# A cycle of 32 scores with four projections, and one MLP job moved from behind the last sums into the attention

## The chip, the core and the metric

The kernel runs on one core of a Trainium2 chip. The metric is the device time of one execution in microseconds (us).

The engines are named as in the profile: PE does the matmuls, ACT (ScalarE) the exponentials, DVE (VectorE) copies and elementwise work, POOL (GpSimd) a little of that, SP issues the transfers. PE writes into PSUM, in banks of 128 x 512 numbers.

## The reference

Two layers of attention and a token-mixing MLP, each with a residual and a layer norm; 2048 tokens, 512 channels, 32 heads of 16 that share one key and value head.

```python
def _A_ref(x, wq, wk, wv, wo):
    q = (x @ wq).reshape(B, S, H, Dh)      # H = 32, Dh = 16
    k = x @ wk
    v = x @ wv
    scores = einsum("bhqd,bkd->bhqk", q, k) * (Dh ** -0.5)
    p = softmax(scores, axis=-1)
    o = einsum("bhqk,bkd->bhqd", p, v)
    return o.reshape(B, S, H * Dh) @ wo

def _B_ref(x, w1, b1, w2, b2):             # F = 1792
    h = layernorm(x)
    u = gelu(einsum("bsd,sf->bdf", h, w1) + b1)
    return einsum("bdf,fs->bsd", u, w2) + b2

for _ in range(2):
    x = x + _A_ref(layernorm(x), wq, wk, wv, wo)
    x = x + _B_ref(layernorm(x), w1, b1, w2, b2)
```

## The kernel before

**Scores and sums.** The attention of a layer is cut into 32 groups (4 heads by 512 queries). A group has 32 steps, each for 128 keys and two heads: two score matmuls into a PSUM pair `sc` (L900; three such pairs exist and are used in turn), an exponential on ACT into a tile `p` (L910), and the sums, matmuls of `p` with the values into the group's accumulator `acc` (L916; two rows of the program, four matmuls in the profile). Some scores are "copied": DVE copies `sc` into `p` first (L908), which frees the pair, and ACT takes the exponential from there. The accumulators of even and odd groups lie in two PSUM banks; the bank that the present group doesn't use is free for other products. When a group's sums are done, DVE empties the accumulator (`ev`, L818), a transfer brings that into `o` (L823), and a division (a reciprocal at L836 and three more operations on each of four columns) makes `hl`.

**What else PE does meanwhile.** Two kinds of other work are laid between scores and sums. A *projection* (`po`, L877) multiplies `hl` with `wo` for 128 tokens: 6 matmuls for two parts `hl`, or 3 (a short one) for one part; DVE adds the result to `x` (L885). Four projections come due at a time, after every fourth group; after those of a token block's last heads the rows of `x` are normalized for the MLP on DVE (L1105 to L1119). A *job* (`pu`, L1187) is one product of the MLP's first matrix, 12 matmuls in two halves (`first`, `second`), after which DVE adds it to `ua` (L1195) and splits the next weights `w` (L1172, L1174). All jobs that the attention doesn't take are done behind it, in `Mixer.rest`; `KEPT` sets how many are kept back for that.

**The order** is written as turns: tuples in which a number above zero computes so many scores (13 and 12: three and two, the last of them copied), 0 does the next part (a projection or half a job), and a number below zero sums so many steps. `Attention.run` takes one turn after the other; `Mixer.turn` chooses it by what is due. `COPIED` is a cycle of 16 steps with two parts, `DOUBLE` one of 32 with four halves (two jobs). After each group of sums in these, `mix.step` puts a limited amount of side work on DVE (division columns, normalization): `room` is the limit, 2.4 in `COPIED` and 1.0 in `DOUBLE`. Engines work through their instructions in the order in which this code emits them.

**Behind the sums** (`rest`), PE does the remaining jobs but eight (`pu_e`), then three of the eight in part (`pu_a`, `pu_m`), while the last `acc` is emptied, moved to `o` and divided (L858 to L860); then the last projections (`po_l`) need that division.

In the layer's late part, four projections come due at the steps 422, 550, 678, 806 and 934 (groups 13, 17, 21, 25, 29), where two `COPIED` cycles follow each other; at step 982 (group 30, and on into 31) four short projections take two `COPIED` cycles, and behind them there is only `PLAIN` (two scores, two sums) to the end of the attention. Two `pu_e` jobs are left for `rest`. Both layers have the same late part.

Of the kernel before, what the change touches and what calls it, by code (L numbers as in the profile page):

```python
# [20 lines left out]
NB = 4  # L21
QB = 512
NG = 8
NKT = S // P
# [8 lines left out]
KEPT = 6  # L33
# [4 lines left out]
WHOLE = (13, 0, 0, 13, -4, 13, -4, 13, -4)  # L38
LONG = (2, 0, 13, -4, 13, -4, 13, 0, 13, -4, 12, -4)
COPIED = (13, 0, 12, 0, 13, -4, 13, -4, 3, -4, 2, -4)  # L40
DOUBLE = (
    13, -4, 13, 0, 0, 13, -4, 13, -4, 13, -4, 13, 0, 13, -4, 13, -4, 12, 0, 13, -4, 13, -4,
)
SHORT = (2, 0, 3, -4, 3, -4)
TINY = (2, 0, 2, -4)
# [21 lines left out]
def kernel(  # L67
# [18 lines left out]
    def pool(name, bufs=1, side="left"):  # L86
        return tc.alloc_tile_pool(name=name, bufs=bufs, side=side, reuse_waits="tile")
# [9 lines left out]
    def bank(i, name):  # L97
        return ps.tile([P, QB], F32, tag=f"ac{i % 2}", name=name)
# [140 lines left out]
    class Proj:  # L239
# [113 lines left out]
        def turn(self, ts_):  # L353

            self.transposes(ts_)
            self.first_rows(ts_)
            self.second_rows(ts_)
# [279 lines left out]
        def later(self, att):  # L637
# [3 lines left out]
            def put(turn, parts):  # L641
                work.append((turn, parts, None))
# [139 lines left out]
    class Attention:  # L782
# [185 lines left out]
        def size(self, turn):  # L968
            return sum(k % 10 for k in turn if k > 0)
# [6 lines left out]
        def run(self, mix, proj):  # L976


            total = 2 * NKT * NG * NB
            guards = [2 * NKT * g for g in sorted({2 * FIRST[self.l], NG})] + [total]  # L980
            self.guards = guards
            later, guarded, flagged = proj.later(self), 0, 0

            rest = range(NB - 2 if self.l == 0 else NB - 1, NB)
            turn, queued = FIRST_TURN[self.l], False
            parts = [lambda i, b=b: proj.values(b, i) for b in rest]
            while self.scored < total:
                mix.chores(self)
                ahead = min(t for t in guards if t > self.scored)
                if ahead < total and self.scored >= ahead - 16 and flagged < ahead:  # L990
                    flagged = ahead
                    proj.flag(proj.flagged)
                if turn is None:
                    turn = PLAIN
                    self.lag = 2 * LAG if mix.normed and self.scored < total - 16 else LAG
                    if len(self.pend) == self.lag:
                        after, queued = None, bool(later) and not mix.projections
                        if queued:
                            turn, parts, after = later[0]
                            if turn is WHOLE and self.to_boundary() >= 14 and self.slack(later) >= 4:  # L1000
                                turn = LONG
                        else:
                            turn, parts = mix.turn(self)
                            if turn is COPIED and not self.spares:
                                turn = LONG
                    left = min(t - self.scored for t in guards if t > self.scored)
                    if queued and turn is LONG and left < self.size(LONG):
                        turn = WHOLE
                    if left < self.size(turn):
                        turn = PLAIN  # L1010
                        if parts and mix.projections and left >= sum(k for k in SHORT if k > 0):
                            turn, parts = SHORT, parts[:1]
                    if turn in (LONG, COPIED) and self.to_boundary() in (2, 4, 2 * NKT):
                        turn = PLAIN
                    if turn is WHOLE and self.to_boundary() == 2:
                        turn = PLAIN
                parts = list(parts)
                for k in turn:
                    if k > 0:
                        self.more(mix, k)  # L1020
                    elif k == 0:
                        if queued and turn is TINY:
                            mix.step(2.0, self)
                        parts.pop(0)(self.spare())
                        if turn is DOUBLE and len(parts) % 2:
                            mix.step(1.0, self)
                        if queued and not parts:
                            later.pop(0)
                            if after:
                                after()  # L1030
                            if not later:
                                proj.close()
                                mix.open()
                    else:
                        if turn is PLAIN:
                            k = -min(4, max(0, len(self.pend) - self.lag))
                        end = self.to_boundary() <= -k
                        busy = self.behind
                        if busy:
                            self.behind = None  # L1040
                            busy()
                        self.drain(-k)
                        mix.chores(self)
                        if busy and turn is not DOUBLE:
                            continue
                        if self.pieces:
                            self.pieces.pop(0)()
                        elif turn in (LONG, COPIED, DOUBLE, WHOLE):
                            room = 2.4 if turn is COPIED else 1.0
                            mix.step(min(room, 0.8 * self.to_boundary()), self)  # L1050
                        elif end:
                            mix.step(2.0, self)
                assert self.scored < guards[-2] or not later
                if self.scored in guards[:-1] and self.scored > guarded:
                    guarded = self.scored
                    i = guards.index(guarded)
                    proj.guard(guarded // (2 * NKT), guards[i + 1] // (2 * NKT))
                    if mix.opened:
                        self.spares = pool(f"more{self.l}")
                if turn is PLAIN and self.to_boundary() > 4:  # L1060
                    mix.step(2.4, self)
                turn = None


    class Mixer:
# [140 lines left out]
        def turn(self, att):  # L1206

            def projection(i):
                self.projection(att, i)

            def first(i):
                self.pu = bank(i, f"pu{self.l}_{self.done}")
                self.product(self.pu, stop=False)
                self.following()

            def second(_):
                r, f = self.product(self.pu, start=False)
                self.add(self.pu, r - 1, f)
                att.behind = self.following

            if len(self.projections) > 1:
                return COPIED, [projection] * 2
            if self.projections:
                return SHORT, [projection]
            early = att.spares and att.scored < 2 * NKT * (NB * NG - 2)
            if early and self.ready(KEPT + 1, 2) and att.to_boundary() in (26, 28, 30):
                return DOUBLE, [first, second] * 2
            return (COPIED, [first, second]) if self.ready(KEPT) else (PLAIN, [])

# [207 lines left out]
        def after(self, s):  # L1437
            self.split2(2 * s + 4)
# [9 lines left out]
    att = Attention(0)  # L1448
# [105 lines left out]
    for layer in range(2):  # L1554
# [63 lines left out]
        if more:  # L1618
# [17 lines left out]
            second = proj.queries(b - 1, 1)  # L1636
# [22 lines left out]
            att = Attention(1)  # L1659
# [36 lines left out]
```

## Time and profile before

| | |
|---|---|
| time, median of 3 runs | 2524.74 us (2522.61 to 2526.94) |
| the profiled execution: time, span | 2526.74 us, 2525.0 us |
| granted clock of PE | 0.997 |
| the late groups of layer 0 (9 to 31) | about 336.8 to 1046.3 us |
| the same of layer 1 | about 1589.9 to 2299.2 us |
| `ev<-acc` copies on DVE | 64, 686 ns each |
| `p<-sc` copies on DVE | 577, 1224 ns each |
| exponentials on ACT from `sc`, from `p` | 1471 of 1046 ns, 577 of 1081 ns |

A row of the timeline gives the start and the length of an instruction, or of a run of equal ones (x6: six of them), and in brackets how long its engine sat idle before it and who released it. The lengths of matmuls overlap; the distance between the starts of two blocks does not. "Scored step 422" is the 423rd step of a layer.

### The profile page before, as it was taken

What the parts mean: (1) busy time and instruction counts of PE and PEld (TensorE: products, weight loads), DVE (VectorE), ACT (ScalarE), POOL (GpSimd) and SP (SyncE); (2) the same over time, 40 slices, a digit from 0 to 9 for tenths busy, and PEclk for the clock granted to TensorE, in tenths of its full rate; (3) what the DMA queues carried; (4) which work ended last, traced back from release to release, by engine and by line L of the source; (5) the groups of instructions that cost most, each with busy time, mean ns of one, the idle gap of its engine ahead of it and who ended that gap; (6) DMA issues with size and microseconds to landing.
All of it is one profiled execution on the core that took longest, in us unless ns stands there. A gap on an engine that the chain in (4) does not pass through costs nothing. (4 is left out here: it accounts for less than half of the span.)

```text
span 2525.0 us, 41934 instructions
## 1 busy us (share of the span) xinstructions
PE 2503.0 (99%) x16158; PEld 1239.1 (49%) x16158; DVE 1520.1 (60%) x2423; ACT 2105.9 (83%) x2348; POOL 151.1 (6%) x239
## 2 busy tenths in 40 slices
PE   9999999999999999999999999999999999999999
PEld 6344334444444444588864443344444444435887
DVE  6565566667666776464544664666676666755532
ACT  6999999999999999653349999999999999995511
POOL 5000000000000000141000000000000000002300
PEclk9999999999999999999999999999999999999999
DMA  3221201111111111144423211111111111102343
GB/s 116 74 64 44 65 26 41 31 39 33 39 31 39 31 39 31 40 113 148 123 62 117 58 47 48 31 39 31 41 31 39 31 43 33 40 22 66 111 124 95
DMA packets 168679, 143.56 MB, mean 57 GB/s; under 512 B 17650, under 2 KB 132368, under 8 KB 167952
## 3 DMA queue, kind: packets, MB, share of 16 engines
q1 hardware_dynamic: 168464, 140.72, 19.2%
q8 instruction: 132, 2.16, 0.4%
q14 instruction: 83, 0.68, 0.1%
HBM read 97.67 MB, written 26.22 MB: 49 GB/s over the span
## 5 line engine op out<-in xcount | busy, mean ns | idle before, releaser
L910 ACT ACTIVATE p<-sc 128x1024 f32<-128x1024 f32 x1471 | 1427.9, 1046 | 73.1 <-PE sc L900 72.0
L916 PE MATMUL acc<-p,vaug 128*32 128x512 f32 x8192 | 1003.1, 600 | 0.8 <-DVE q L519 0.8
L908 DVE COPY p<-sc 128x1024 f32<-128x1024 f32 x577 | 706.4, 1224 | 483.2 <-PE sc L900 433.3
L900 PE MATMUL sc<-qs,kst 51*128 51x512 f32 x4096 | 690.0, 433 | 10.6 <-ACT p L910 3.7
L910 ACT ACTIVATE p<-p 128x1024 f32<-128x1024 f32 x577 | 623.5, 1081 | 11.9 <-DVE p L908 6.6
L900 PEld LDWEIGHTS sc<-qs,kst 51*128 51x128 f32 x4096 | 336.7, 185 | 577.6 <-ACT p L910 400.2
L916 PEld LDWEIGHTS acc<-p,vaug 128*32 128x32 f32 x8192 | 217.6, 109 | 487.0 <-issue 470.9
L1427 PE MATMUL py<-u,w 128*128 128x512 f32 x1344 | 307.4, 390 | 0.0
L1427 PEld LDWEIGHTS py<-u,w 128*128 128x128 f32 x1344 | 251.8, 188 | 52.3
L1415 ACT CAST w<-w2r 128x896 fp32r<-128x896 f32 x64 | 60.3, 945 | 184.8 <-PE py L1427 177.1
L1187 PE MATMUL pu<-hb,w 128*128 128x512 f32 x768 | 204.6, 407 | 0.0
L1174 POOL TENSOR_TENSOR w<-w1r,w 128x256 fp32r<-128x256 f32 x90 | 72.8, 817 | 1586.7 <-ACT w L1172 1585.7
L1187 PEld LDWEIGHTS pu<-hb,w 128*128 128x128 f32 x768 | 136.2, 188 | 58.4 <-issue 31.6
L1416 DVE TENSOR_TENSOR w<-w2r,w 128x896 fp32r<-128x896 f32 x64 | 72.0, 1125 | 111.4 <-ACT w L1415 111.1
L818 DVE COPY ev<-acc 128x512 f32<-128x512 f32 x64 | 43.9, 686 | 142.1 <-PE acc L916 142.1
L836 DVE RECIPROCAL o<-o 128x128 f32<-128x128 f32 x120 | 113.4, 945 | 9.5 <-DMA o<-ev 9.5
L877 PE MATMUL po<-wo,hl 128*128 128x512 f32 x360 | 100.5, 412 | 2.0 <-DVE x L885 0.3
L406 PE MATMUL pq<-hT,wq 128*128 128x512 f32 x312 | 81.4, 404 | 0.0
L877 PEld LDWEIGHTS po<-wo,hl 128*128 128x128 f32 x360 | 62.6, 188 | 34.8 <-DVE x L885 12.0
L1172 ACT CAST w<-w1r 128x256 fp32r<-128x256 f32 x90 | 36.0, 406 | 51.7 <-PE pu_l L1187 14.0
L1187 PE MATMUL pu_l<-hb,w 128*128 128x512 f32 x336 | 77.1, 389 | 0.0
L1433 DVE SCALAR_TENSOR_TENSOR x<-py,b2c,x 128x512 f32<-128x512 f32 x32 | 24.0, 750 | 81.2 <-PE py L1427 81.2
(191 smaller groups left out, 1189.3 us busy)
## 6 DMA issues: line engine op xcount, KB each, us to landing
w1r<-in_B_w_dram SPq DMA_DIRECT2D x224, 128.0 KB
w2r<-in_B_w_dram SPq DMA_DIRECT2D x64, 448.0 KB
qs<-qd SPq DMA_DIRECT2D x384, 64.0 KB
qd<-q SPq DMA_DIRECT2D x64, 256.0 KB
o<-ev SPq DMA_DIRECT2D x128, 128.0 KB
x<-in_A_x_dram SPq DMA_DIRECT2D x16, 256.0 KB
hd<-hT SPq DMA_DIRECT2D x2, 2048.0 KB
out_dram<-x SPq DMA_DIRECT2D x16, 256.0 KB
```

Source lines behind the costliest of these rows:

```text
L406: yield nc.tensor.matmul(out, a, c, start=(k == 0), stop=(k == len(terms) - 1))
L836: nc.vector.reciprocal(o[:, 1, c], o[:, 1, c])
L877: nc.tensor.matmul(po, a, c, start=(k == 0), stop=(k == 3 * len(parts) - 1))
L900: nc.tensor.matmul(sc[:, j, :], kst[kt // 4][rows, kt % 4 * P : (kt % 4 + 1) * P], qs[i % NQ][rows, j0 // 2, :], start=True, stop=True,)
L908: nc.vector.tensor_copy(pt, sc)
L910: nc.scalar.activation(pt, sc, AF.Exp, scale=0.25)
L916: nc.tensor.matmul(self.acc[i][c : c + 32, :], vaug[:, kt].rearrange("p d k -> p (d k)"), pt[:, j, :], start=(kt == 0), stop=(kt == NKT - ...
L1174: eng.tensor_tensor(w[:, 1], raw, f32(w[:, 0]), op=ALU.subtract)
L1187: nc.tensor.matmul(pu, a, c, start=(start and k == 0), stop=(stop and k == 5))
L1415: nc.scalar.copy(w[:, 0], raw)
L1416: nc.vector.tensor_tensor(w[:, 1], raw, f32(w[:, 0]), op=ALU.subtract)
L1427: nc.tensor.matmul(py, a, d, start=(c == 0 and f == 0 and k == 0), stop=(c == 1 and f == NFH - 1 and k == 2),)
```

## The change

Two turns are added. `QUAD` is one cycle of 32 with four projections, taken in place of two `COPIED` cycles where four projections are due and 26, 28 or 30 steps of the group are still to be summed. `ENDING` is a cycle of 32 with three projections, a whole job and a fourth projection, taken where four are due with 14 steps left, which is at step 982. The side work's limit is 2.4 in `QUAD` and 1.0 in `ENDING`.

```diff
+QUAD = (13, -4, 13, 0, 3, -6, 13, 0, 13, -4, 3, -4, 12, 0, 13, 0, 13, -6, 13, -4, 13, -4)
+ENDING = (
+    13, 0, -2, 13, -2, 0, 13, -4, 13, 0, 12, -6, 3, 0, 0, 13, -4, 13, 0, -2, 13, -4, 13, -4, 13, -4,
 )
...
-                        elif turn in (LONG, COPIED, DOUBLE, WHOLE):
-                            room = 2.4 if turn is COPIED else 1.0
+                        elif turn in (LONG, COPIED, DOUBLE, QUAD, ENDING, WHOLE):
+                            room = 2.4 if turn in (COPIED, QUAD) else 1.0
...
+            early = att.spares and att.scored < 2 * NKT * (NB * NG - 2)
+            early = early and att.to_boundary() in (26, 28, 30)
+            if early and len(self.projections) > 3:
+                return QUAD, [projection] * 4
+            if len(self.projections) > 3 and att.to_boundary() == 14 and self.ready(KEPT):
+                return ENDING, [projection] * 3 + [first, second, projection]
             if len(self.projections) > 1:
                 return COPIED, [projection] * 2
             if self.projections:
                 return SHORT, [projection]
-            early = att.spares and att.scored < 2 * NKT * (NB * NG - 2)
-            if early and self.ready(KEPT + 1, 2) and att.to_boundary() in (26, 28, 30):
+            if early and self.ready(KEPT + 1, 2):
                 return DOUBLE, [first, second] * 2
```

In each layer five pairs of `COPIED` become a `QUAD`, and the pair at step 982 becomes an `ENDING`; nothing else is chosen differently. The lines of the changed file are four to nine further down than those of before.

PE, group 13, from the third score of the first triple on, before (`po_4_0` is the projection of the parts `hl_4`, `hl_5` for the first 128 tokens):

```order
L900 MATMUL sc_13_4_0_5474<-qs_90,kst_85 128x512 x2
L877 MATMUL po_4_0_5480<-wo_1151,hl_4_4628 128x512 x3
L877 MATMUL po_4_0_5480<-wo_1151,hl_5_5238 128x512 x3
L900 MATMUL sc_13_4_2_5488<-qs_90,kst_85 128x512 x2
L900 MATMUL sc_13_5_0_5493<-qs_90,kst_85 128x512 x2
L877 MATMUL po_4_1_5499<-wo_1151,hl_4_4628 128x512 x3
L877 MATMUL po_4_1_5499<-wo_1151,hl_5_5238 128x512 x3
L900 MATMUL sc_13_5_2_5507<-qs_90,kst_85 128x512 x2
```

and now:

```order
L904 MATMUL sc_13_4_0_5474<-qs_90,kst_85 128x512 x2
L920 MATMUL acc_13_5456<-p_13_1_0_5414,vaug 32x512 x2
L920 MATMUL acc_13_5456<-p_13_1_2_5434,vaug 32x512 x2
L920 MATMUL acc_13_5456<-p_13_2_0_5439,vaug 32x512 x2
L920 MATMUL acc_13_5456<-p_13_2_2_5444,vaug 32x512 x2
L904 MATMUL sc_13_4_2_5488<-qs_90,kst_85 128x512 x2
L904 MATMUL sc_13_5_0_5493<-qs_90,kst_85 128x512 x2
L904 MATMUL sc_13_5_2_5498<-qs_90,kst_85 128x512 x2
L881 MATMUL po_4_0_5504<-wo_1151,hl_4_4628 128x512 x3
L881 MATMUL po_4_0_5504<-wo_1151,hl_5_5238 128x512 x3
```

Two projections stood two scores apart; now four sums and three scores come before the first one, and the second one (not shown) follows after two triples of scores and six sums.

PE, groups 30 and 31, around the end of group 30's sums, before:

```order
L900 MATMUL sc_31_2_0_10924<-qs_90,kst_84 128x512 x2
L900 MATMUL sc_31_2_2_10929<-qs_90,kst_84 128x512 x2
L916 MATMUL acc_30_10654<-p_30_15_0_10880,vaug 32x512 x2
L916 MATMUL acc_30_10654<-p_30_15_2_10885,vaug 32x512 x2
L916 MATMUL acc_31_10943<-p_31_0_0_10890,vaug 32x512 x2
L916 MATMUL acc_31_10943<-p_31_0_2_10904,vaug 32x512 x2
L900 MATMUL sc_31_3_0_10948<-qs_90,kst_84 128x512 x2
```

and now:

```order
L920 MATMUL acc_30_10659<-p_30_15_0_10884,vaug 32x512 x2
L920 MATMUL acc_30_10659<-p_30_15_2_10898,vaug 32x512 x2
L904 MATMUL sc_31_2_0_10944<-qs_90,kst_84 128x512 x2
L904 MATMUL sc_31_2_2_10949<-qs_90,kst_84 128x512 x2
L904 MATMUL sc_31_3_0_10954<-qs_90,kst_84 128x512 x2
L1191 MATMUL pu_64_10959<-hb_8_9366,w_0_64_10339 128x512 x3
L1191 MATMUL pu_64_10959<-hb_9_9403,w_0_64_10339 128x512 x3
L1191 MATMUL pu_64_10959<-hb_10_9876,w_0_65_10687 128x512 x3
L1191 MATMUL pu_64_10959<-hb_11_9899,w_0_65_10687 128x512 x3
```

The job with the weights `w_0_64` and `w_0_65`, before the first `pu_e` behind the last sums, now stands here; behind the sums the one with `w_0_66` and `w_0_67` is left.

DVE, the end of group 18, up to the copy of the score `sc_19_4_0`; group 17's projections were followed by a normalization. Before (reciprocal and three operations: a division column of `o_16`; `ev_18` empties group 18's accumulator):

```order
L836 RECIPROCAL o_16_6654<-o_16_6654 128x128
L840 TENSOR_TENSOR o_16_6654<-o_16_6654 128x128
L841 CAST hl_8_7142<-o_16_6654 128x128
L842 TENSOR_TENSOR hl_8_7142<-o_16_6654,hl_8_7142 128x128
L818 COPY ev_18_7303<-acc_18_6987 128x512
L908 COPY p_19_4_0_7326<-sc_19_4_0_7323 128x1024
```

and now:

```order
L840 RECIPROCAL o_16_6655<-o_16_6655 128x128
L822 COPY ev_18_7298<-acc_18_6969 128x512
L844 TENSOR_TENSOR o_16_6655<-o_16_6655 128x128
L845 CAST hl_8_7243<-o_16_6655 128x128
L846 TENSOR_TENSOR hl_8_7243<-o_16_6655,hl_8_7243 128x128
L840 RECIPROCAL o_16_6655<-o_16_6655 128x128
L844 TENSOR_TENSOR o_16_6655<-o_16_6655 128x128
L845 CAST hl_8_7243<-o_16_6655 128x128
L846 TENSOR_TENSOR hl_8_7243<-o_16_6655,hl_8_7243 128x128
L912 COPY p_19_4_0_7328<-sc_19_4_0_7325 128x1024
```

Between the emptying and the copy there stood nothing; now the rest of one column and one whole column stand there.

More of the change, by code (lines that the diff above doesn't have):

```diff
@@ L42 @@
     13, -4, 13, 0, 0, 13, -4, 13, -4, 13, -4, 13, 0, 13, -4, 13, -4, 12, 0, 13, -4, 13, -4,
+)
+QUAD = (13, -4, 13, 0, 3, -6, 13, 0, 13, -4, 3, -4, 12, 0, 13, 0, 13, -6, 13, -4, 13, -4)
+ENDING = (
+    13, 0, -2, 13, -2, 0, 13, -4, 13, 0, 12, -6, 3, 0, 0, 13, -4, 13, 0, -2, 13, -4, 13, -4, 13, -4,
 )
```

## The prediction

> **What bounds the kernel now.** I read the page's busy times first, then the timeline of TensorE alone, then the windows by stretch.
>
> ```profile
> PE 2503.0 (99%) x16158; PEld 1239.1 (49%) x16158; DVE 1520.1 (60%) x2423; ACT 2105.9 (83%) x2348; POOL 151.1 (6%) x239
> ```
>
> PE says 99%, but a matmul's row runs on until the next one starts, so this share cannot tell work from waiting; what can is the time from one block's start to the next one's. A "block" below is an unbroken run of score matmuls (sc), sums (acc), a projection (po) or half a job (pu). This is the timeline of PE over the two cycles of 16 with projections (columns: start in us, length, engine, line, operation), with the first block of the cycle after as its last row:
>
> ```profile
> 464.85 0.96 PE L900 MATMUL sc<-qs,kst 51*128 51x512 f32 x6
> 465.75 1.66 PE L877 MATMUL po<-wo,hl 128*128 128x512 f32 x6
> 467.34 0.88 PE L900 MATMUL sc<-qs,kst 51*128 51x512 f32 x4
> 468.19 1.66 PE L877 MATMUL po<-wo,hl 128*128 128x512 f32 x6
> 469.77 0.97 PE L900 MATMUL sc<-qs,kst 51*128 51x512 f32 x6
> 470.67 1.92 PE L916 MATMUL acc<-p,vaug 128*32 128x512 f32 x16
> 472.52 0.96 PE L900 MATMUL sc<-qs,kst 51*128 51x512 f32 x6
> ...
> 496.19 0.50 PE L900 MATMUL sc<-qs,kst 51*128 51x512 f32 x2
> ```
>
> From start to start: three scores (x6) 0.90, a projection 1.59, four sums (x16) 1.85. The two cycles take 496.19 - 464.85 = 31.34 us. Shorter blocks stand at the end of the attention, where two scores and two sums alternate:
>
> ```profile
> 1038.30 0.73 PE L900 MATMUL sc<-qs,kst 51*128 51x512 f32 x4
> 1038.96 1.06 PE L916 MATMUL acc<-p,vaug 128*32 128x512 f32 x8
> 1039.96 0.73 PE L900 MATMUL sc<-qs,kst 51*128 51x512 f32 x4
> ```
>
> Two scores take 0.66, two sums 1.00; so two more sums in a block cost 0.85, and six take 1.85 + 0.85 = 2.70. A cycle of 32 of the kind that the change copies exists already, with two jobs in the place of four projections (24 other matmuls in both):
>
> ```profile
> 403.69 0.96 PE L900 MATMUL sc<-qs,kst 51*128 51x512 f32 x6
> ...
> 407.33 3.03 PE L1187 MATMUL pu<-hb,w 128*128 128x512 f32 x12
> 410.30 0.97 PE L900 MATMUL sc<-qs,kst 51*128 51x512 f32 x6
> ...
> 434.27 0.50 PE L900 MATMUL sc<-qs,kst 51*128 51x512 f32 x2
> ```
>
> It takes 30.58. Its blocks sum to 10 x 0.90 + 0.66 + 8 x 1.85 + 2.97 (x12) + 2 x 1.59 = 30.61, 0.03 over by rounding. So PE runs there without a wait, and a cycle costs what its blocks cost. The same sum for the two projection cycles is 8 x 0.90 + 4 x 0.66 + 8 x 1.85 + 4 x 1.59 = 31.00 against 31.34: over 0.3 us of waiting, of which the x4 block at 467.34 shows 0.85 - 0.66 = 0.19 (the second po needs the bank that the first one's addition empties), and there are two such places. The windows show how full the others are (length, then busy time of each engine):
>
> ```profile
> core 0: us, PE busy (x) PEld busy (x) DVE busy (x) ACT busy (x) POOL busy (x), PEclk, DMA share, GB/s
> 464.85:496.19 31.34, 31.22 (x222) 12.69 (x218) 14.12 (x17) 30.72 (x34) 0.00 (x0) 1.00 0.08 23
> 585.60:616.95 31.35, 31.23 (x220) 12.70 (x218) 25.77 (x58) 30.74 (x34) 0.00 (x0) 1.00 0.09 27
> 403.69:434.27 30.58, 30.58 (x221) 12.90 (x218) 18.68 (x26) 29.83 (x34) 0.00 (x0) 1.00 0.13 40
> 1005.30:1035.79 30.49, 29.72 (x209) 10.82 (x206) 14.07 (x17) 29.87 (x33) 0.00 (x0) 1.00 0.03 9
> ```
>
> ACT is close behind PE, but at 30.58 it still keeps up with 32 exponentials. DVE is loaded unevenly: 14 us in one pair, 26 in another.
>
> **The cycle of four projections (ten times, five in each layer).** Its blocks are 10 x 0.90 + 0.66 + 5 x 1.85 + 2 x 2.70 + 4 x 1.59 = 30.67, less the 0.03 of the sum above 30.64, against 31.34: two blocks fewer, and three scores or more stand between any two projections, so that the 0.19 waits go. Gain 0.70 each, 7.0 us in all. What could take it back is ACT, which must finish 32 exponentials in 30.64; it does that in 30.58 in the row above. Bounds: at best the 30.58 (7.6 in all), at worst only the waits go (3.8).
>
> **Work on DVE that slides into the next cycle (four times).** The new cycle has seven places where VectorE gets side work, the two old ones eight. Two of the five in a layer carry a normalization (the pair at 585.60), so one division column more is left for the stretch before the cycle of 32 that follows. There the trace of before has:
>
> ```profile
> 645.32 0.95 DVE L836 RECIPROCAL o<-o 128x128 f32<-128x128 f32 x1
> ...
> 647.10 0.95 DVE L836 RECIPROCAL o<-o 128x128 f32<-128x128 f32 x1
> ...
> 649.59 0.69 DVE L818 COPY ev<-acc 128x512 f32<-128x512 f32 x1 [0.63 <-PE acc L916]
> 651.38 1.23 DVE L908 COPY p<-sc 128x1024 f32<-128x1024 f32 x1 [1.10 <-PE sc L900]
> ```
>
> A column is 647.10 - 645.32 = 1.78; DVE's idle time here is 0.63 + 1.10 = 1.73. But the 0.63 lies ahead of ev, which stands before the last column and a third; behind ev there come about 2 us (0.69 + 0.8 + 1.78 less the overlap), so the score copy starts near 652.3, not 651.38. It ends at 653.5, and PE wants that buffer three scores later, after four sums and two scores of a block begun at 650.3: about 653.6. I take 0.3 us for each of the four, 1.2 in all; bounds 0 and 1.0 each.
>
> **The cycle in the last group but one (twice).** It gets a job (x12) more. Before, the two short cycles begin:
>
> ```profile
> 1005.30 0.98 PE L900 MATMUL sc<-qs,kst 51*128 51x512 f32 x6
> 1006.21 0.95 PE L877 MATMUL po<-wo,hl 128*128 128x512 f32 x3
> 1007.09 0.49 PE L900 MATMUL sc<-qs,kst 51*128 51x512 f32 x2
> 1007.90 0.50 PE L900 MATMUL sc<-qs,kst 51*128 51x512 f32 x2 [0.32 <-ACT p L910]
> ...
> 1035.79 0.73 PE L900 MATMUL sc<-qs,kst 51*128 51x512 f32 x4
> ```
>
> They take 30.49, though their blocks sum to only 8 x 0.90 + 4 x 0.66 + 8 x 1.85 + 4 x 0.88 = 28.16: here PE waits 2.3 us, mostly for ACT (the second score starts 0.81 after the first, not 0.33). That is the room the job goes into. The new cycle's blocks are 10 x 0.90 + 0.66 + 5 x 1.85 + 2.70 + 3 x 1.00 + 4 x 0.88 + 2.97 = 31.10; one place has a short projection between three and two scores as at 1007.09, which I price at 0.5. So 31.6 against 30.49: 1.1 more, 2.2 for both layers. Sums that follow a projection directly, three edges in this cycle, stand nowhere in the trace; the overhead of a block bounds them, 0 to 0.2 each. Bounds 0.6 to 1.9 a layer. Here the Trainium skill bears on the reading: "Trainium Kernel Development and Optimization", section Best Practices, says that matmul busy share is no measure of how near PE is to its limit. By that rule the block sum is right and the busy column wrong, and the trace agrees: 29.72 busy stands over 28.16 of work. By the busy column the room would be 30.49 - 29.72 = 0.77, and the job's 2.97 would cost 4.4 in the two layers instead of 2.2.
>
> **One job fewer behind the sums (twice).** PE's rows there, and what the first projection behind them needs:
>
> ```profile
> 1047.38 5.74 PE L1187 MATMUL pu_e<-hb,w 128*128 128x512 f32 x24
> 1052.95 2.88 PE L1187 MATMUL pu_a<-hb,w 128*128 128x512 f32 x12
> 1055.67 5.60 PE L1187 MATMUL pu_m<-hb,w 128*128 128x512 f32 x24
> 1061.11 0.63 PE L877 MATMUL po_l<-wo,hl 128*128 128x512 f32 x2
> ...
> 1053.76 0.95 DVE L858 RECIPROCAL o<-o 128x128 f32<-128x128 f32 x1
> ...
> 1060.19 0.29 DVE L855 TENSOR_TENSOR hl<-o,hl 128x128 fp32r<-128x128 f32 x1 [0.16 <-ACT hl L860]
> ...
> 1048.21 1.11 SPq L823 DMA_DIRECT2D o<-ev  x2
> ...
> 309.50 1.20 SPq L823 DMA_DIRECT2D o<-ev  x2
> 313.01 0.95 DVE L836 RECIPROCAL o<-o 128x128 f32<-128x128 f32 x1 [5.22 <-DMA o<-ev]
> ```
>
> Twelve matmuls take 1055.67 - 1052.95 = 2.72, back to back, and nothing else of the job was on the path: 5.44 for both layers. The job was also cover: the division (6.7 us from its first reciprocal to its last split) stood behind it. It can start when o has landed, 3.51 us after its issue (309.50 to 313.01): 1051.72, so its last column is done at 1058.45. PE comes to po_l at 1058.39 and needs the first column then, the last one three projections later. So it stays hidden; were the transfer 1 us later, up to 1 us a layer would show.
>
> **Sum.** -7.0 + 1.2 + 2.2 - 5.4 = -9.0 us. Against the profiled execution (2526.74, its span 2525.0) that is 2517.7; the median of the three runs is 2.0 lower, 2524.74, and gives 2515.7, my forecast. By the bounds it goes from -7.6 + 0 + 1.2 - 5.4 = -11.8 to -3.8 + 4.0 + 3.8 - 3.4 = +0.6. Some 0.2%, 5 us, is what a measurement of this kernel can tell from none.
>
> **Rivals.** (1) *ACT paces the new cycle*: nine scores of it are copied, eight before, and ACT is busy for 30.72 of 31.34. Only the two 0.19 waits go, 3.8 in all, and the sum is -5.8: 2518.9. For it: ACT has 0.6 us of idle time. Against: 29.83 in the cycle with two jobs, which copies eleven. (2) *The job finds no room before the last group*: PE's 2.4 us there are ACT's, and the job's 2.97 come on top of 30.49. The two layers lose 5.9 where I charge 2.2: -5.3, 2519.4. Against: an exponential may run while PE does the job. (3) *Slower: VectorE's queue.* A score copy waits behind whatever side work was put ahead of it; if that makes PE wait one division column (1.78) in each new cycle, ten of them cost 17.8, and with the 1.2 taken out the sum is -9.0 - 1.2 + 17.8 = +7.6: 2532.3. From 1.02 us per cycle on there is no gain left, and from 1.5 on it is slower by what can be measured. For it: 25.77 us of DVE work in the pair at 585.60. Against: three of five pairs have 14. The Trainium skill's "TensorE: Matmul & The Clock Gate", section on the 16 sub-arrays, has VectorE as a strict FIFO, which speaks for this case; the trace cannot show otherwise, since DVE's rows stand in program order.
>
> **How the numbers follow.** Forecast 0.66, rival (1) 0.13, (2) 0.10, (3) 0.06, several small misses that cancel the gain 0.05. Predicted 2515.7. Range 2511 to 2521: below, the best bound (2512.9) and the 2 us by which the runs of before lie under their median; above, rivals (1) and (2) and as much spread; outside are (3), the cancelling case and the ends of the forecast, about 0.15. Faster by over 0.2%: the forecast 0.66 and half of (1) and (2), which lie near the edge: 0.78. Within: the other half and most of the cancelling case, 0.16. Slower: (3), 0.06.
>
> **What would show it.** Right: each projection cycle 30.6 from score to score with no x4 block of 0.85; the last group but one near 31.5; pu_e x12 at 2.8 and po_l 2.7 us closer to the last sums, with no idle time of PE before it. Wrong: [<-DVE p L908] on scores in or behind the new cycles (3), idle before scores from ACT there (1), 33 us or more in the last group but one (2), or PE waiting at po_l for DVE.

## The result

The changed kernel takes 2519.69 us (median of 14 runs, 2516.19 to 2521.31); the kernel before, in the same series, 2524.2 us (2520.25 to 2526.94). The ratio is 0.9984 with a 95% interval of 0.9977 to 0.9991: 4 to 5 us are gained, about half of the 9.0 forecast, and with 0.16% just inside the 0.2% from which on I had called it faster (I had given this outcome 0.16). The profiled execution has a span of 2518.5 us, before 2525.0.

The page's first line shows nothing of this. PE's share is the same 99%, ACT has four instructions fewer, DVE 22 more:

```profile
PE 2497.5 (99%) x16158; PEld 1239.9 (49%) x16158; DVE 1538.4 (61%) x2445; ACT 2104.5 (84%) x2344; POOL 148.7 (6%) x235
```

What shows it is the distance from start to start, by stages. These are sums over both layers, in us, from the PE timelines of the profiled executions. "Behind new cycles" is the cycle with two jobs that begins at scores 614 and 902, one or two cycles of 32 after a new one; the two last columns are the first two experiments below.

| stage | before | after | four projections only | ending only |
|---|---|---|---|---|
| ten cycles with four projections | 313.65 | 308.21 | 308.59 | 313.64 |
| four cycles behind new cycles (614, 902) | 122.34 | 124.56 | 124.61 | 122.28 |
| last group but one, twice | 60.97 | 63.62 | 60.92 | 63.63 |
| `pu_e`, twice | 11.15 | 5.75 | 11.14 | 5.75 |
| `pu_m`, twice | 10.88 | 11.66 | 10.88 | 11.65 |
| sum of these | 518.99 | 513.81 | 516.15 | 516.95 |
| all other stages from score 422 on | 1126.53 | 1126.61 | 1126.81 | 1126.29 |
| scores 0 to 421 of both layers | 835.32 | 833.79 | 834.17 | 832.39 |

So the edit is worth -5.2 us in the stages that it touches, all other late stages agree to 0.3, and the first 422 scores, whose code is the same, wander by 3 us (the granted clock has a share in that; see the last section).

**The new cycle** (PE timeline of after, the first cycle in layer 0, and the first block of the next):

```profile
465.27 0.96 PE L904 MATMUL sc<-qs,kst 51*128 51x512 f32 x6
466.16 1.92 PE L920 MATMUL acc<-p,vaug 128*32 128x512 f32 x16
468.02 0.96 PE L904 MATMUL sc<-qs,kst 51*128 51x512 f32 x6
468.90 1.65 PE L881 MATMUL po<-wo,hl 128*128 128x512 f32 x6
470.49 1.16 PE L904 MATMUL sc<-qs,kst 51*128 51x512 f32 x6
471.57 2.78 PE L920 MATMUL acc<-p,vaug 128*32 128x512 f32 x24
...
496.06 0.96 PE L904 MATMUL sc<-qs,kst 51*128 51x512 f32 x6
```

It takes 496.06 - 465.27 = 30.79, forecast 30.64. One block is too long: the triple at 470.49 takes 1.08 instead of 0.89. The same moment with the other engines says why:

```profile
469.79 1.07 ACT L914 ACTIVATE p<-sc 128x1024 f32<-128x1024 f32 x1
470.49 0.18 PEld L904 LDWEIGHTS sc<-qs,kst 51*128 51x128 f32 x2 [0.36 <-issue]
470.91 0.30 PEld L904 LDWEIGHTS sc<-qs,kst 51*128 51x128 f32 x4 [0.24 <-ACT p L914]
```

The second score starts at 470.91 because the exponential that frees its pair of banks ends at 469.79 + 1.07 = 470.86. Between the starts of the two triples lie only three scores and a projection, 2.47 us, and three exponentials take 2.76 (ACT begins those of the triple at 468.02 at 468.88, and the next three at 471.64). In the cycle with two jobs of before, ACT came to its triples early, since it waits for scores behind the twelve matmuls of a job:

```profile
410.90 1.94 ACT L910 ACTIVATE p<-sc 128x1024 f32<-128x1024 f32 x2 [0.67 <-PE sc L900]
```

**The cycle at 614** (all engines, layer 0). The last division columns stand ahead of the score copy at 652.08, and the third score waits for it:

```profile
649.63 0.97 PE L904 MATMUL sc<-qs,kst 51*128 51x512 f32 x6
650.30 0.94 DVE L840 RECIPROCAL o<-o 128x128 f32<-128x128 f32 x1
...
652.08 1.22 DVE L912 COPY p<-sc 128x1024 f32<-128x1024 f32 x1
652.38 0.73 PE L904 MATMUL sc<-qs,kst 51*128 51x512 f32 x4
653.33 1.06 ACT L914 ACTIVATE p<-p 128x1024 f32<-128x1024 f32 x1 [1.16 <-DVE p L912]
653.35 0.49 PE L904 MATMUL sc<-qs,kst 51*128 51x512 f32 x2 [0.23 <-DVE p L912]
```

This triple takes 653.77 - 652.38 = 1.39 (a job begins at 653.77) instead of 0.89: 0.5 us, and ACT sits idle for 1.16.

**The last group but one** (PE timeline, from 1012.23 on; the cycle begins at 1003.88):

```profile
1012.23 0.97 PE L904 MATMUL sc<-qs,kst 51*128 51x512 f32 x6
1013.12 0.96 PE L881 MATMUL po<-wo,hl 128*128 128x512 f32 x3
1014.01 0.49 PE L904 MATMUL sc<-qs,kst 51*128 51x512 f32 x2
1014.92 0.50 PE L904 MATMUL sc<-qs,kst 51*128 51x512 f32 x2 [0.41 <-ACT p L914]
1015.35 2.78 PE L920 MATMUL acc<-p,vaug 128*32 128x512 f32 x24
...
1035.69 0.73 PE L904 MATMUL sc<-qs,kst 51*128 51x512 f32 x4
```

From 1003.88 to 1035.69 it is 31.81 (forecast 31.6); the block of two scores takes 1015.35 - 1014.01 = 1.33, twice the usual 0.66.

**Behind the sums** (all engines, layer 0; the PEld row is from that engine's own timeline):

```profile
1047.28 3.04 PE L1191 MATMUL pu_e<-hb,w 128*128 128x512 f32 x12
1050.16 2.88 PE L1191 MATMUL pu_a<-hb,w 128*128 128x512 f32 x12
1051.68 0.95 DVE L862 RECIPROCAL o<-o 128x128 f32<-128x128 f32 x1 [0.64 <-DMA o<-ev]
1052.88 5.99 PE L1191 MATMUL pu_m<-hb,w 128*128 128x512 f32 x24
...
1056.20 0.30 ACT L864 CAST hl<-o 128x128 fp32r<-128x128 f32 x1 [1.00 <-DVE o L863]
1056.41 0.40 ACT L1176 CAST w<-w1r 128x256 fp32r<-128x256 f32 x1
1056.89 0.74 POOL L1178 TENSOR_TENSOR w<-w1r,w 128x256 fp32r<-128x256 f32 x1 [0.87 <-ACT w L1176]
1057.68 0.76 PEld L1191 LDWEIGHTS pu_m<-hb,w 128*128 128x128 f32 x4 [0.39 <-POOL w L1178]
1058.71 1.56 PE L881 MATMUL po_l<-wo,hl 128*128 128x512 f32 x6
```

`pu_e` takes 2.88 instead of 5.58. But `pu_m` takes 1058.71 - 1052.88 = 5.83 instead of 5.44: PE waits for the weights of its own jobs. The chain is readable from bottom to top: the weights wait for POOL, POOL for ACT's cast, ACT's cast stands behind the `hl` cast of the division, and that waits 1.00 for DVE, whose first reciprocal waited for the transfer of `o`.

### The profile page after: what moved, and what is told of

It is laid out like the page before. It is cut to its first block, busy times and chain, and to the rows that moved or that the text cites. A ratio compares the mean times of both kernels' runs of the same rounds, so it can differ in the third digit from the quotient of the medians.

```text
span 2518.5 us, 41939 instructions
## 1 busy us (share of the span) xinstructions
PE 2497.5 (99%) x16158; PEld 1239.9 (49%) x16158; DVE 1538.4 (61%) x2445; ACT 2104.5 (84%) x2344; POOL 148.7 (6%) x235
## 5 line engine op out<-in xcount | busy, mean ns | idle before, releaser
L912 DVE COPY p<-sc 128x1024 f32<-128x1024 f32 x591 | 723.3, 1224 | 516.2 <-PE sc L904 445.6
L914 ACT ACTIVATE p<-p 128x1024 f32<-128x1024 f32 x591 | 639.4, 1082 | 16.6 <-DVE p L912 11.3
L1191 PE MATMUL pu<-hb,w 128*128 128x512 f32 x792 | 210.7, 407 | 0.0
```

The costliest lines, as they stand in the source:

```text
L912: nc.vector.tensor_copy(pt, sc)
L914: nc.scalar.activation(pt, sc, AF.Exp, scale=0.25)
L1191: nc.tensor.matmul(pu, a, c, start=(start and k == 0), stop=(stop and k == 5))
```

## The experiments

My theory: four separate terms, each mis-sized by an amount that has a place in the trace. The rivals: the terms hang together (ACT or VectorE is full), or the waits come from elsewhere. Four of the kernels below (division columns later, weights' casts first, the group without its job, sums first) were executed once each; they are read by their stages alone, not by their time.

**The cycle with four projections alone.**

```diff
-            if len(self.projections) > 3 and att.to_boundary() == 14 and self.ready(KEPT):
-                return ENDING, [projection] * 3 + [first, second, projection]
```

> Only the new cycles of 32 with four projections; the last group but one is as before and two jobs are left behind the sums. My theory (the parts add up, each mis-sized by a little): the new cycles take 30.8 to 30.9 each as after (0.53 less than two COPIED, ten of them: -5.3), the two cycles with two jobs at scores 614 and 902 of each layer stay at 31.0 to 31.3 (+0.5 to +0.7 each, +2.3), the last group but one is 30.5, pu_e x24 takes 5.6 and pu_m x24 is back at 5.4 to 5.6: -3.0 us against the kernel before. Rival A (the late VectorE work at 614 and 902 has nothing to do with the new cycles): 614 and 902 at 30.6, -5.3 us. Rival B (the new cycles help only together with the ending): less than -1.5 us.

Measured: 2520.48 us against 2522.29, ratio 0.9993 (0.9983 to 1.0002); the stages give -2.8 (table). The late cycles at 614 and 902 belong to the new cycles: rival A falls. With -2.8, B falls by the stages; the timed interval alone wouldn't exclude it.

**The ending alone.**

```diff
-            if early and len(self.projections) > 3:
-                return QUAD, [projection] * 4
```

> Only the new last group but one with its job; the projections elsewhere stand in pairs of COPIED as before. My theory: that group 31.8 instead of 30.5 (+1.3 a layer), pu_e x12 2.88 instead of x24 5.58 (-2.7), pu_m x24 5.8 instead of 5.4 (+0.4): -1.0 a layer, -2.0 us against the kernel before; 614 and 902 at 30.6 as before. Rival (pu_m is late because the new cycles changed which weights are loaded when, not because of the missing job): pu_m 5.4, -2.8 us.

Measured: 2519.91 against 2522.29, ratio 0.9990 (0.9981 to 0.9999); the stages give -2.0. `pu_m` is late here too, 5.84 and 5.81, so it is the missing job, not the new cycles. The two parts add up to within 0.4: -2.8 and -2.0 against -5.2 for both.

**Division columns later.** Only the slot right ahead of 614 and 902 is cut to one step, and the first slots of the cycle behind 902 are widened, so that two of them take two steps:

```diff
                             room = 2.4 if turn in (COPIED, QUAD) else 1.0
+                            if self.scored in (614, 902) and turn is COPIED:
+                                room = 1.0
+                            elif 902 <= self.scored < 934 and len(mix.steps) > 8:
+                                room = 1.6
```

> As after, but in the cycle ahead of scores 614 and 902 the last slot takes one step of the division instead of three; the other two go into the cycle with two jobs behind it. My theory (a copied score waits in VectorE's queue behind these columns and the copy of ev, and ACT and PE wait for it): 614 goes from 31.06 and 31.32 to 30.6, 902 from 31.14 and 31.05 to 30.6 to 30.8; the x6 blocks of 1.39 there are back at 0.89; -1.7 to -2.3 us against after. Rival A (VectorE has just too much work in that stretch, wherever it stands): the wait turns up at a later triple of the same cycle, 31.1 stays. Rival B (the copy of ev, which isn't moved, is what holds the score copy): 31.1 stays, with the wait at the same triple.

Measured: 614 goes from 31.06 to 30.57 and from 31.32 to 30.82, the triple of 1.39 back to 0.89. So the columns hold the score copy, and the copy of `ev`, which stayed, doesn't. But 902 takes 31.26 and 31.28 instead of 31.13 and 31.05. The wait has moved to the triples around the half job (PE timeline):

```profile
937.34 1.34 PE L904 MATMUL sc<-qs,kst 51*128 51x512 f32 x6
938.61 1.65 PE L1195 MATMUL pu<-hb,w 128*128 128x512 f32 x6
940.19 1.26 PE L904 MATMUL sc<-qs,kst 51*128 51x512 f32 x6
```

940.19 - 938.61 is the 1.58 of a half job; the triples take 1.27 and 1.19. At 902 this is rival A; whether the number of steps or the two in one slot did it, the kernel with one column less below tells.

**The weights' casts first.** Behind the sums each division column is issued half a job later:

```diff
-            next(division)
...
-            for pu, between in zip(going, (division, division, None)):
+            for pu, between in zip(going, (division, division, division)):
                 job(pu, between)
```

(and `next(between, None)`, since the division runs out of steps)

> As after, but behind the sums each column of the last division is issued one half job later, so that ACT has a cast of w weights ahead of the first cast of hl. My theory (the weights' casts stand in ACT's queue behind hl casts that wait for the division, and PE waits for the weights): pu_m x24 goes from 5.83 and 5.80 back to 5.44, nothing new in front of po_l: -0.4 a layer, -0.8 us against after. Rival A (PE waits for the weights' transfer or for GpSimd's subtraction): pu_m stays at 5.8. Rival B (the division is the chain): pu_m 5.44, and PE waits the same 0.4 in front of po_l.

Measured: `pu_m` 5.44 in both layers, -0.78 in all, and 2.78 from `po_l` to the next block as before. The loads of the weights run without a break (PEld's timeline):

```profile
1050.55 5.40 PEld L1191 LDWEIGHTS pu_m<-hb,w 128*128 128x128 f32 x24
1055.98 2.04 PEld L881 LDWEIGHTS po_l<-wo,hl 128*128 128x128 f32 x9
```

Both rivals fall. The transfer and the division begin no earlier against PE than in after; only the order in ACT's queue is another. The Trainium skill's "TensorE: Matmul & The Clock Gate", section on the 16 sub-arrays, calls ScalarE and VectorE strict FIFOs; this run agrees with it for ACT (`pu_m` 5.83 or 5.44 by the order alone), the run before for VectorE (the triple at 614, 1.39 or 0.89).

**The last group but one without its job.**

```diff
-    ... 12, -6, 3, 0, 0, 13, -4, 13, 0, -2, ...
+    ... 12, -6, 3, 13, -4, 13, 0, -2, ...
...
-                return ENDING, [projection] * 3 + [first, second, projection]
+                return ENDING, [projection] * 4
```

> As after, but the last group but one has its four projections and no job; the two jobs stand behind the sums as before. My theory (the job fills time in which PE would wait for ACT, as the prediction had it): this group takes 29.6 to 30.5 instead of 31.8, so that the job costs 1.3 to 2.2 of its 2.97; with pu_e x24 5.6 and pu_m 5.4 behind it the kernel is 0.2 to 2.0 us slower than after. Rival (the prediction's second rival, that the job finds no room): 28.8, the job costs all of its 2.97, and the kernel is some 1.3 us faster than after.

Measured: 32.62 and 31.02 instead of 31.81 and 31.82, with 12 matmuls fewer. Where the job stood, six scores now follow each other, and each of the last three waits for an exponential (PE timeline):

```profile
1016.94 0.97 PE L904 MATMUL sc<-qs,kst 51*128 51x512 f32 x6
1018.62 0.50 PE L904 MATMUL sc<-qs,kst 51*128 51x512 f32 x2 [0.71 <-ACT p L914]
1019.53 0.50 PE L904 MATMUL sc<-qs,kst 51*128 51x512 f32 x2 [0.41 <-ACT p L914]
1020.45 0.80 PE L904 MATMUL sc<-qs,kst 51*128 51x512 f32 x2 [0.42 <-ACT p L914]
```

The block takes 1021.18 - 1016.94 = 4.24 (3.94 in layer 1) instead of 1.79. In layer 0 the sums behind it take 3.17 instead of 1.85 as well. That is no wait but the clock: PE was granted half of it (column PEclk) from 1020.48 to 1023.89:

```profile
core 0: us, PE busy (x) PEld busy (x) DVE busy (x) ACT busy (x) POOL busy (x), PEclk, DMA share, GB/s
1020.48:1023.89 3.41, 3.41 (x18) 0.86 (x18) 1.23 (x1) 2.81 (x3) 0.00 (x0) 0.50 0.02 5
```

Layer 1 has the same three waits at full clock and takes 31.02; with half of the 3.41 us taken off, an estimate, layer 0 takes 30.9. So the job did fill time in which PE would wait: at full clock its 2.94 us cost 0.8 (31.82 - 31.02). The prediction's second rival (28.8) falls; my number for this run was wrong as well, since I hadn't counted what this order loses without a filler.

**Sums ahead of the block of two scores.**

```diff
-    ... 13, 0, 12, -6, 3, 0, 0, ...
+    ... 13, 0, -4, 12, -2, 3, 0, 0, ...
```

> As after, but in the last group but one the six sums behind the block of two scores stand partly ahead of it (four sums, two scores, two sums), so that PE comes to the second of these scores later. My theory (PE waits there for one exponential, 0.67 too much in a block of 1.33, and nowhere else): the block goes to 0.66, a change between kinds of matmul more costs 0.14 to 0.2, and the group takes 31.3 instead of 31.80: -0.5 a layer. Rival (ACT paces the whole cycle, so that the wait turns up at the next scores): 31.8 stays.

Measured: 31.43 in both layers, -0.38 each instead of -0.5. The block takes 0.66, but the triple behind it 1.06 (PE timeline, layer 0):

```profile
1013.23 1.92 PE L921 MATMUL acc<-p,vaug 128*32 128x512 f32 x16
1015.08 0.73 PE L905 MATMUL sc<-qs,kst 51*128 51x512 f32 x4
1015.75 1.07 PE L921 MATMUL acc<-p,vaug 128*32 128x512 f32 x8
1016.74 0.97 PE L905 MATMUL sc<-qs,kst 51*128 51x512 f32 x6
```

(the job begins at 1017.80). 0.17 of the 0.67 came back there, as the rival has it; another 0.13 is the one change more between kinds of matmul (four sums and two take 1.85 + 0.99, six take 2.71).

**Three edits together**: the division columns later, the weights' casts first, and the sums ahead of the block of two scores:

> After with the three edits together: division columns later ahead of 614 and 902, a cast of w weights ahead of the first hl cast behind the sums, and four of the sums ahead of the block of two scores in the last group but one. My theory (three separate waits, that add up): -1.7 to -2.3, -0.8 and -1.0 make -3.5 to -4.1 us against after, 0.996 to 0.998 of the kernel before. Rival (the waits share a cause, VectorE and ACT being full): less than half of that.

Measured: 2517.92 us against 2523.39 of before, ratio 0.9977 (0.9966 to 0.9987). By the stages it is 1.9 us shorter than after, half of what I expected, which is just where the rival begins. Most of the shortfall is 902 (31.28 in both layers), 0.3 the last group but one; the edits came out as they had one by one (-0.6, -0.8 and -0.7; alone -0.6, -0.8 and -0.8), so the waits are separate.

**One column less.** The widened slots are taken out, and the slot ahead of 902 takes two steps instead of one:

```diff
                             if self.scored in (614, 902) and turn is COPIED:
-                                room = 1.0
-                            elif 902 <= self.scored < 934 and len(mix.steps) > 8:
-                                room = 1.6
+                                room = 1.0 if self.scored == 614 else 1.6
```

> The three edits again, but ahead of score 902 the last slot takes two steps (split, invert) and only one split goes into the cycle behind it, none of whose slots is widened. My theory (VectorE needs one step to a slot; a score copy is late only where a slot takes two or more): 902 comes to 30.6 from 31.13 and 31.05, where the kernel with one step there and two in the next cycle's first slots has 31.28; 614 stays at 30.57 and 30.8, the last group but one at 31.45, pu_m at 5.44: -1.6, -0.8, -0.7 make -3.1 us against after by the stages. Rival (the reciprocal with the split is too much in that slot however it's cut, since the copy of ev stands there too): 902 at 30.9 to 31.1, -2.3 us.

Measured: 902 takes 30.58 and 30.57; 2514.3 us against 2523.7, ratio 0.9963 (0.9949 to 0.9977); by the stages 3.4 us less than after, 3.1 expected. The triple that took 1.41 there takes 0.89, with a reciprocal still ahead of its copy, and from the next slot on one step to a slot:

```profile
922.29 0.95 DVE L841 RECIPROCAL o<-o 128x128 f32<-128x128 f32 x1
...
923.15 1.16 DVE L913 COPY p<-sc 128x1024 f32<-128x1024 f32 x1
924.38 0.96 PE L905 MATMUL sc<-qs,kst 51*128 51x512 f32 x6
```

Leaving out one split of 0.8 us, less than half a column, was enough. So VectorE's load as such wasn't the matter.

**The new cycle begun elsewhere** in the same round, with the weights' casts and the sums edited as above and no edit of the slots:

```diff
-QUAD = (13, -4, 13, 0, 3, -6, 13, 0, 13, -4, 3, -4, 12, 0, 13, 0, 13, -6, 13, -4, 13, -4)
+QUAD = (12, 0, 13, 0, 13, -6, 13, -4, 13, -4, 13, -4, 13, 0, 3, -6, 13, 0, 13, -4, 3, -4)
```

> The edits of the division's casts and of the last group but one as before, none on the slots, and the new cycle begun at another place of the same round: two scores, projection, three scores, projection, and the six sums ahead of the plain triples. The projections then come earlier, and with them the norm steps and the division columns behind them, so that none stands in the last slot ahead of 614 and 902. My theory (PE waits 0.19 in each new cycle because ACT is 0.26 behind when the first projection follows a triple; behind a pair or six sums it is not): the block of 1.06 to 1.11 goes to 0.89 and the new cycle takes 30.6, what the prediction had; 614 at 30.6 and 902 at 30.6 too; against after -1.9 (ten cycles), -2.0 (614 and 902), -0.7, -0.8: -5.4 us, 0.996 of the kernel before. Rival (ACT paces the cycle as a whole, the prediction's first rival): the wait comes back at another triple, the cycle stays at 30.8, and 3.5 us are gained.

Measured: 2521.32 us, ratio 0.9993 (0.9984 to 1.0002): the forecast fell. Its own mechanism held: the cycles at 422 and 934 take 30.62 to 30.68, what the prediction had, and 614 and 902 need no edit any more (30.57, but 30.82 at 614 of layer 1). PE timeline of the first:

```profile
461.73 0.73 PE L905 MATMUL sc<-qs,kst 51*128 51x512 f32 x4
462.39 1.65 PE L882 MATMUL po<-wo,hl 128*128 128x512 f32 x6
463.97 0.96 PE L905 MATMUL sc<-qs,kst 51*128 51x512 f32 x6
464.87 1.65 PE L882 MATMUL po<-wo,hl 128*128 128x512 f32 x6
466.45 0.96 PE L905 MATMUL sc<-qs,kst 51*128 51x512 f32 x6
...
492.35 0.73 PE L905 MATMUL sc<-qs,kst 51*128 51x512 f32 x4
493.40 0.50 PE L905 MATMUL sc<-qs,kst 51*128 51x512 f32 x2 [0.32 <-ACT p L915]
```

But the first block behind the new cycle takes 1.48 to 1.53 where the last row shows its wait, and the cycles behind the ten new ones take 6.1 us more together; and the cycles at 550 and 806, with normalization in their slots, take 31.17 to 31.22 (678 takes 31.06 in layer 0, 30.70 in layer 1).

**The last triple copied.**

```diff
-QUAD = (..., 13, 0, 13, -4, 3, -4)
+QUAD = (..., 13, 0, 13, -4, 13, -4)
```

> As the kernel before it (pair first), but the last triple of the new cycle is copied too. My theory (the first block of the cycle behind the new one takes 1.48 to 1.51 instead of 0.89 because the plain triple ahead of it gives its last bank pair back only after the third exponential): 454, 710, 838 and their likes go from 31.2 to 30.56, 582 from 31.63 to 31.05, 966 from 16.1 to 15.5, so 0.6 for each of ten, 6 us less than pair first, 2515.3; the waits of 1.15, 1.18 and 1.33 in the new cycles at 550, 678 and 806 stay, where norm steps take VectorE. Rival (it is ACT that is behind after this order of the round, whoever copies): the blocks of 1.5 stay near 1.2 to 1.5 and 2520 or more is measured.

Measured: 2517.32 us, ratio 0.9982 (0.9973 to 0.9991). The first blocks are back at 0.88 to 0.90 (one, 454 of layer 1, at 1.11), so the plain triple was their cause. But only the cycles at 454 and 710 are as short as expected (30.57 to 30.79); those at 838, 582 and 966 still take 31.0, 31.7 and 15.72. At 838 and 582 a score copy stands behind normalization steps that this order moves there, and ACT waits 0.75 for it (layer 0, copies at 865.30 and 618.78). At 966 it is the wait of the new cycle again: the blocks of scores at 986.53 and 989.01 begin 2.48 apart, and the second score of the later one waits for an exponential. The order saves 0.15 us in a cycle without side work and loses more next to VectorE's.

**The changed kernel and the best one, side by side** (the kernel with one column less is run again unchanged).

> The changed kernel once more, on the same chip as the next one. My theory: 0.9975 to 0.9992 of the kernel before, the stages as in its first profile to 0.1 us, the first 422 scores of a layer anywhere between 411 and 421 us. Rival (its 4.5 us were a matter of that chip): 0.9995 or more.

> The kernel with the three edits and one column less ahead of 902 once more. My theory (its stages are 3.1 us shorter than after's, and the rest of its lead of 5 us was the run-to-run spread of the first 422 scores): 2.5 to 3.7 us less than the changed kernel on the same chip. Rival (the first 422 scores are faster in it): 4.5 us less or more.

Measured: 2518.51 us (ratio 0.9983, 0.9974 to 0.9992) and 2514.53 us (0.9965, 0.9952 to 0.9979), against 2523.0 of before. The stages of after came out as in its first profile, sum 513.90 against 513.81; those of the best are 510.45. The best kernel is 4.0 us shorter, of which the stages explain 3.5; the remaining 0.5 lies within the spread of the first 422 scores (833.48 in the profile of after, 832.03 in that of the best).

## Why the prediction was half right

The mechanism held in all four parts. What failed were sizes, all on the same side: -9.0 was forecast, the stages give -5.2. The time alone would have misled: 2519.69 lies inside the range, but nearest to the second rival's 2519.4, which the runs refute.

- **The cycle of four projections, -7.0: measured -5.4.** The step that failed is "three scores or more stand between any two projections, so that the 0.19 waits go". Those two went. But a new one of the same size came: a triple behind a triple and a projection waits 0.19 for an exponential. My bound, that ACT keeps up in the cycle with two jobs, was read from the total, in which ACT has its rest behind the twelve matmuls of a job (the 0.67 us above); here nothing that long stands ahead of the triple. That is the first rival in small: ACT doesn't pace the cycle (30.62 was measured with as many exponentials), it paces one place.
- **Side work that slides, +1.2: measured +2.2**, 0.5 each and 0.2 more in layer 1 at 614. That 0.2 is the wait of the new cycle at another place: behind a triple and half a job, 2.50 us after the triple before, stands a triple of 1.08 (at 1915.90), whose second score starts at 1916.31, behind an exponential that ends at 1916.26. In layer 0 ACT is 0.28 us further there, and the triple takes 0.89. The place, the engine and the row were those that I had named. What failed is "the score copy starts near 652.3", 2.0 us behind the cycle's first score at 650.3: it started 2.45 us behind it (652.08 - 649.63), and PE waits accordingly. The copy of `ev`, a split and a column sum to 3.27 from the start of `ev`; the prediction let 2.71 of that stand, for overlap, and 3.17 was measured. By its own figures (copied at 653.5, wanted at 653.6) there was no wait at all, so the 0.3 was a guess. It is the third rival's mechanism, but in four cycles and not in ten.
- **The last group but one, +2.2: measured +2.7.** Priced for the block of two scores behind a short projection were 0.5; it took 0.67 over. Edges between projections and sums cost nothing that I could see.
- **One job fewer, -5.4: measured -5.4, but +0.8 beside it.** "It stays hidden" was right of `po_l` and wrong of what else stood under the same cover. I followed DVE's columns to the projection that needs them, not ACT's queue, where casts of the weights of `pu_m` stand behind casts of `hl`. With the 2.72 us of cover gone, 0.39 us of waiting in each layer showed, for which no row of before had a sign.

These four make up the 3.8 us by which the stages fall short of the forecast. That 4.0 us lie between 2515.7 and 2519.69 is nearly the same number by chance: the forecast started from 2524.74, the kernel before came out at 2524.2, and the first 422 scores differ from profile to profile.

## What to carry to other kernels

Where a tuned kernel's cycles cost what their blocks cost, a new cycle's price is its blocks plus what each buffer's way back allows: for every block, reckon the distance to the block that used the same buffer last, not the engine's total over the cycle. When work is taken from behind a wait, list every queue that was covered by it; here the engine that waited was not the one that the division feeds. And a wait of half a microsecond that is found in a row can be undone by a small change of the order: three such edits brought 3.5 us by the stages, where the change itself brought 5.2. Before a long block is called a wait, look at the granted clock over it.

## What the runs showed of the hardware

All late stages outside the change sum to 1126.3 to 1126.8 us wherever the new round wasn't moved, and most cycles with the same instructions repeat to 0.05 us from profile to profile. Some triples behind a triple and six matmuls of a job jump: the one at score 472 of layer 1 took 0.88 to 0.90 in most profiles and 1.08 or 1.09 in two (the kernel with four projections only, and the one without a job).

The first 422 scores, the same instructions in every kernel here, took 829.5 to 835.3 us in both layers together. Most of the spread between profiles arises there, and a difference of 3 us between two totals says nothing until this stretch is taken out. Much of it is the granted clock. In the profile of before it is 0.50 for 6.83 us at the first scores of layer 0, and again for 6.83 us from 1307.91 on, in layer 1:

```profile
48.39:55.22 6.83, 6.29 (x27) 1.93 (x28) 3.88 (x9) 4.42 (x5) 0.94 (x1) 0.50 0.52 134
```

Two sums take 1.86 in it instead of 1.00. In the 14 profiles such stretches, of 3.41 or 6.83 us, make up between nothing (the new cycle begun elsewhere, 829.5 us) and 13.7 us (before, 835.3) of these scores. With half of that time taken off, an estimate, they take 827.3 to 829.5 us everywhere: 2.2 us of spread instead of 5.8. What sets such a stretch off wasn't tried. In the kernel without its job one follows three waits of PE in layer 0, but none follows the same waits in layer 1.
